# Softmax denominators in three PSUM rows per head group instead of one, in a fused attention and MLP kernel

## The chip, the cores and the metric

The kernel runs on one core of one Trainium2 chip. The metric is the device time of one execution in microseconds (us). Engines are called as in the profile: PE (TensorE matmuls), PEld (TensorE weight loads), DVE (VectorE), ACT (ScalarE), POOL (GpSimd), SP (SyncE).

## What is computed

Forgetting attention over 8 batches of 8 heads, 576 positions, head dimension 64, and then a two-layer MLP with a tanh GELU over the 4608 rows of 512 features that come out of it.

```
scores = scale * q @ k.T;  cum = cumsum(log(clip(f, 1e-4, 1)))
attn   = exp(where(causal, -1e9, scores + cum_i - cum_j) - max)
out    = (attn / (sum(attn) + 1e-9)) @ v          # per head
y      = gelu_tanh(x @ w_in) @ w_out              # x: the heads side by side
```

The kernel keeps the exponentials `pt` with keys on partitions and queries along the columns. The decay of a key is a weight per key, `w`; it multiplies the values (`vw`), and the denominator of a query is the sum over keys of `w * pt`, a matmul with the single column `w_bf` as its weights.

## The kernel before

**Head groups.** The work of attention is cut into 16 groups of 4 heads (quads), i = 0 to 15; quad i belongs to batch i // 2. A quad's exponentials lie in `pt[i % 2]`, 128 partitions x 4 heads x 1536 columns. The causal triangle is cut into six pieces by blocks of keys (`low`, 0, 1, 2, 3, `high`), of 64, 512, 448, 320, 192 and 64 query columns: 1600 columns per head.

**Steps of a quad**, by the names of the order tables:
- S.i.r (L264): scores of one of three rounds of 512 columns, matmuls at L282, with the four heads in four row strips of TensorE, and the exponential on ACT at L290.
- M.i.r (L292): the causal mask by selects on POOL (L296), one per diagonal block. M.i.2 issues two of them, first that of key block 2, then that of key block 3. m.i.r does the same on DVE (L326).
- D.i (L361): the denominators. `product` (L330, matmuls at L352) sends 6 pieces x 4 heads = 24 matmuls, the four heads in four column strips of TensorE, into PSUM row 32 * h of tile `po`: one useful row per head, 576 columns wide. For pieces 0 and `low` the weight column is repeated 32 times, so that all 32 rows of a head have a number; for the others it is one column. Then DVE transposes all 576 columns in 32 x 32 blocks from PSUM to `den` (L371), takes the reciprocal of 18 values per partition (L373), and spreads them back to 32 rows per head by a second transpose into `rb` (L375).
- V.i.x (L379): the weighted values, again 24 matmuls at L352 in the same shapes, and on DVE the product with `rb` into `xT` (L384). x = 0 and 1 are the even and odd features.

Quads 0 and 1 are done in two parts of 256 and 320 queries, D.0.p and V.0.x.p, with matmuls at L338 into tile `po_m`; they have 2 and 5 pieces.

**The order** is written out by hand. The tables FRONT, SECOND, STEADY, FLUSH and LAST (L71 on) list words that are issued in sequence; every engine takes its instructions in that order. Between the steps of attention stand pieces of the MLP for rows that are ready: F and f (second layer, L616; f sends it in four column strips of 32), I and i (first layer, L400), Q (first layer by seven products, L536). From quad 6 on, two quads go with one chunk of 512 rows, and the order around a pair is

```
S.3.0 X G.1.1.2 f.0.16 M.3.0 D.2 VW.3 f.0.12 S.3.1 M.3.1 V.2.0 f.0.13
S.3.2 M.3.2 CL.3 V.2.1 VW.4 f.0.15 S.4.0 D.3 f.0.10 V.3.0 M.4.0 CL.4
```

with 2 and 3 standing for the chunk's even quad (which was masked in the turn before) and its odd quad. So M.3.2, the last mask of the odd quad, is issued to POOL one S, one V and some f ahead of D.3.

**PSUM.** `po` is the only buffer of its pool (`psO`, L347), which D, V and some first-layer products share; `po_m` takes one of two buffers of `psM` (L334).

Of the kernel before, what the change touches and what calls it, by code (L numbers as in the profile page):

```python
# [8 lines left out]
FP32 = mybir.dt.float32  # L9
# [7 lines left out]
def kernel(  # L17
# [10 lines left out]
    nc = tc.nc  # L28

    B, H, S, D = q.shape  # L30
# [20 lines left out]
    pieces = [  # L51
        ("low", 0, 0, 64),
        (0, 64, 64, 512),
        (1, 576, 128, 448),
        (2, 1024, 256, 320),
        (3, 1344, 384, 192),
        ("high", 0, 512, 64),
    ]
    QA = 256
    split_rounds = [(1152, 384), (0, 512), (512, 320), (832, 384)]  # L60
    split_pieces = [
        [(0, 1152, 0, 256), (1, 1408, 128, 128)],
        [(0, 0, 256, 320), (3, 320, 384, 192)],
        [(1, 512, 256, 320)],
        [(2, 832, 256, 320), ("high", 1152, 512, 64)],
    ]
    LOW, HIGH = NT, NT - 1
# [1 line left out]
    ON_ACT = ()  # L69

    FRONT = """  # L71
        LP.1 LP.4 SC LP.0 WI.0 B.8.512 B.1.512 CT TK.0 CE.1 TQ.0 CE.0 B.2.512 LP.3 B.1.128 BK.0.2 B.1.512 WI.5 B.1.512 S.0.0 TK.1 M.0.0 B.1.128
        B.1.128 WI.1 WI.2 B.1.128 BK.0.1 B.3.512 H.0.2.1 B.1.128 BK.0.1 H.0.2.0 WI.3 H.0.1.0 W.0 LP.2 TQ.1 D.0.0 H.1.0.0 vw.0.0 B.1.128 B.2.512
        BK.1.1 H.1.0.1 M.1.0 H.0.1.1 B.1.512 M.0.1 vw.1.0 V.0.1.0 B.1.128 B.1.512 V.0.0.0 H.0.3.0 UT D.1.0 j.0.0.4 V.1.0.0 V.1.1.0 H.1.3.1 WI.4 WI.7
        H.0.3.1 WI.6 j.0.0.4 j.0.0.8 H.1.1.0 RJ.0.0 M.0.3 WO.0 H.1.1.1 vw.0.1 LC.1.1 D.0.1 j.0.1.8 H.1.3.0 M.1.1 WO.1 M.1.3 H.1.2.1 V.0.0.1 VW.1.1
        V.0.1.1 UW.2.1 W.1 LQ.2 H.1.2.0 J.0.2 LK.2 LK.3 WO.2 D.1.1 j.0.1.8 GJ.0.1 V.1.0.1 V.1.1.1 TK.2 J.0.3 tr WO.3 J.1.1 TQ.2 GJ.0.0 LQ.3 U.0
        J.1.3 J.1.2 J.1.0 F.0.1 f.0.3 LC.1.2 LC.1.0 f.0.2 S.2.0 TK.3 X f.0.2 PW.2.2 F.0.7 LC.1.3 F.0.1 S.2.2 f.0.2 F.0.1 TQ.3 f.0.2 LC.1.4 LQ.4 LK.5
        f.0.4 S.2.1 F.0.1 f.0.4 LV.2.1 F.0.1 LK.4 F.0.3 M.2.2 F.0.1 vw.2 m.2.1 F.0.2 CL.2 LV.2.0 S.3.0 f.0.1 M.2.0 f.0.2 D.2 f.0.3 S.3.1 TQ.4 f.0.1
        LQ.6 VW.3 f.0.4 M.3.0 f.0.1 V.2.0 TK.4 S.3.2 f.0.6 V.2.1 m.3.1 S.4.1 f.0.4 LQ.5 f.0.1 H.4.2.0 f.0.2 M.3.2 H.4.2.1 cl.3 D.3 VW.4 H.4.0.0
        M.4.2.3 H.4.0.1 V.3.1 LK.6 v.3.0 f.0.1 F.0.1 I.1.2 I.1.0 TQ.5 U.1 TK.5 TQ.6 vw.5 I.1.5 UW.2.4 I.1.1 LV.3.1 LV.3.0 I.1.3 TK.6 U.3 I.1.4 U.2  # L80
        m.4.2.2 I.1.6 I.1.7 LK.7 X F.1.1 CL.5 F.1.2 M.4.1 G.0 G.1.1.2 F.1.4 cl.4 F.1.9 S.5.0 F.1.12 UW.2.3 m.4.0 F.1.4 M.5.0 F.1.4 F.1.5 S.5.1 D.4
        F.1.5 LQ.8 F.1.2 F.1.4 S.5.2 V.4.0 f.1.1 M.5.1 M.5.2.2 M.5.2.3 LK.8 f.1.11 V.4.1 S.6.0 f.1.3 D.5 LQ.7@m.3.1 M.6.0 f.1.10 S.6.1 vw.6 f.1.1
        V.5.1 f.1.1 F.1.9 CL.6 M.6.1 F.1.2 S.6.2 m.6.2.3 f.1.1 V.5.0 f.1.4 F.1.2 m.6.2.2
    """

    SECOND = """
# [27 lines left out]
    den_pool = ctx.enter_context(tc.tile_pool(name="den", bufs=2))  # L114
    psS = ctx.enter_context(tc.tile_pool(name="psS", bufs=2, space=bass.MemoryType.PSUM))
    psO = ctx.enter_context(tc.tile_pool(name="psO", bufs=1, space=bass.MemoryType.PSUM))
    psM = ctx.enter_context(tc.tile_pool(name="psM", bufs=2, space=bass.MemoryType.PSUM))

    def many(n, shape, dtype, name):
        return [singles.tile(shape, dtype, name=f"{name}{i}") for i in range(n)]  # L120
# [11 lines left out]
    vw = many(2, [128, NT + 1, 4, D], BF16, "vw")  # L132
    pt = many(2, [128, 4, 3 * 512], BF16, "pt")
# [14 lines left out]
    w_bf = singles.tile([128, NQ, NT + 1, 4], BF16, name="w_bf")  # L148
# [12 lines left out]
    for u in range(4):  # L161
        if u not in wsum:
            n = 3 * len([x for x in wsum if x not in UNIT_LIST])
# [38 lines left out]
    parts = [(0, QA), (QA, S)]  # L202
# [127 lines left out]
    def product(i, groups, spare, part=None):  # L330
        p = pt[i % 2]
        if part is not None:
            s0, s1 = parts[part]
            po = psM.tile([128, 512], FP32, name="po_m", tag="m")  # L334
            for (key, col, q0, nq) in sorted(sum(split_pieces[1:] if part else split_pieces[:1], []), key=lambda x: HIGH if x[0] == "high" else x[0]):
                for (r0, lhsT, h) in groups:
                    w = lhsT(HIGH if key == "high" else key)
                    nc.tensor.matmul(  # L338
                        po[r0:r0 + w.shape[-1], q0 - s0:q0 - s0 + nq], w, p[:, h, col:col + nq],
                        start=(key == 0), stop=(key == (HIGH if part else 1)),  # L340
                        skip_group_check=True,
                    )
            return po[:, 0:s1 - s0]
        if spare:
            po = psS.tile([128, 2, 512], FP32, name="ps_o", tag="s").rearrange("p a n -> p (a n)")
        else:
            po = psO.tile([128, 1024], FP32, name="po", tag="po")  # L347
        for (key, col, q0, nq) in sorted(pieces, key=lambda x: {0: 0, "low": 1}.get(x[0], 2)):
            t = {"low": LOW, "high": HIGH}.get(key, key)
            for (r0, lhsT, h) in groups:  # L350
                w = lhsT(t)
                nc.tensor.matmul(  # L352
                    po[r0:r0 + w.shape[-1], 448 + q0:448 + q0 + nq], w, p[:, h, col:col + nq],
                    start=(key in (0, "low")), stop=(key in ("low", "high")),
                    skip_group_check=True,
                )
        return po[:, 448:448 + S]
# [2 lines left out]

    def denominators(i, part=None):  # L361

        def column(h):

            return lambda t: (w_bf[:, i, t, h:h + 1] if t not in (0, LOW) else
                              w_bf[:, i, t, h:h + 1].to_broadcast([128, 32]))

        po = product(i, [(32 * h, column(h), h) for h in range(4)], False, part)
        n = S if part is None else parts[part][1] - parts[part][0]
        den = den_pool.tile([128, S], FP32, name="den", tag="den")  # L370
        nc.vector.transpose(out=den[:, 0:n], in_=po)  # L371
        rec = den_pool.tile([128, S // 32], FP32, name="rec", tag="rec")
        nc.vector.reciprocal(rec[:, 0:n // 32], den[:, 0:n:32])  # L373
        rb = den_pool.tile([128, S], FP32, name="rb", tag="rb")
        nc.vector.transpose(out=rb[:, 0:n].rearrange("p (c j) -> p c j", j=32),  # L375
                            in_=rec[:, 0:n // 32].unsqueeze(2).to_broadcast([128, n // 32, 32]))
        rbs[i, part] = rb[:, 0:n]
# [398 lines left out]
    def load_values(b, half):  # L776
# [9 lines left out]
        "M": lambda i, r, *keys: mask(i, r, keys),  # L786
        "m": lambda i, r, *keys: mask_by_product(i, r, keys),
        "D": denominators,
        "V": lambda i, x, *part: attn_out(i, x, False, *part),
        "v": lambda i, x, *part: attn_out(i, x, True, *part),  # L790
# [98 lines left out]
```

## Time and profile before

| what | us |
|---|---|
| median of 3 runs (range) | 322.77 (321.95 to 322.95) |
| the profiled execution's own time | 322.02 |
| its span, first to last instruction | 320.1 |
| PE busy in it | 311.8 |
| DVE busy in it | 242.5 |
| granted TensorE clock | 1.00 throughout |

In the rows of the profile, the first number of a line of the timeline or of the chain is the start in us from the span's start, the second its length in us. "x24" is a count of instructions. "128*32" is a weight tile of 128 rows and 32 columns. What stands in brackets is idle time before the row, with what ended it. In the rows of one group, "busy, mean ns" comes before the bar's idle time.

### The profile page before, as it was taken

To read this page: it belongs to the slowest core of one execution; us is meant where nothing else is said; L and a number is where in the kernel's file an instruction comes from. 1 tells how busy PE (TensorE), PEld (TensorE's weight loads), DVE (VectorE), ACT (ScalarE), POOL (GpSimd) and SP (SyncE) were. 2 spreads that over 40 slices of the span, in tenths; PEclk is the share of its full clock that TensorE was granted. 3 is DMA by queue.
4 is the path that set the end of the run, shared out by engine and by line. 5 is a ranking of instruction groups with operands and counts; after the bars stand their busy time and mean duration, and the time that the engine had idled before them with its cause. 6 is when DMAs were issued, how large, how long until landed. Compare 5 with 4: busy or idle time off the path is not lost.

```text
span 320.1 us, 11762 instructions
## 1 busy us (share of the span) xinstructions
PE 311.8 (97%) x5301; PEld 219.1 (68%) x5318; DVE 242.5 (76%) x369; ACT 212.9 (67%) x246; POOL 109.9 (34%) x148
## 2 busy tenths in 40 slices
PE   6899999999999999999999999999999999999996
PEld 2367734545676577776788878767776786688785
DVE  7667528598878889879877987699876865597674
ACT  3766885966766876877677866787686744836610
POOL 8799541830340417311850075206610140000000
PEclk9999999999999999999999999999999999999999
DMA  7999999985253901693149411961011110100203
GB/s 127 227 197 204 208 222 223 171 153 105 51 99 100 215 9 39 137 190 72 39 97 218 84 39 44 218 137 38 5 60 40 35 39 33 35 33 2 100 33 99
DMA packets 47491, 33.41 MB, mean 104 GB/s; under 512 B 29777, under 2 KB 42193, under 8 KB 47441
## 3 DMA queue, kind: packets, MB, share of 16 engines
q0 software_dynamic: 9632, 15.99, 29.1%
q1 hardware_dynamic: 37664, 16.60, 19.4%
q8 instruction: 41, 0.67, 0.9%
q14 instruction: 10, 0.07, 0.1%
q10 hardware_dynamic: 144, 0.07, 0.1%
HBM read 36.85 MB, written 9.44 MB: 145 GB/s over the span
## 4 chain that ended last, share of the span: by engine, by line
PE 91%; DMA 3%; ACT 2%; POOL 1%; DVE 1%; issue 1%; DVEq 0%; POOLq 0%
PE ps_w L616 30%; PE ps_h L400 19%; PE po L352 9%; PE ps_s L282 9%; PE ps_q L536 8%; PE pso L685 5%; PE ps_h L436 5%; PE ps_u L484 4%; DMA v_nat<-in_v_dram 3%; PE po_m L338 1%; ACT gT L408 1%; ACT pt L290 1%; POOL v_nat L183 0%; PE ps_o L352 0%; PE ps_p L616 0%
## 5 line engine op out<-in xcount | busy, mean ns | idle before, releaser
L290 ACT ACTIVATE pt<-ps_s 128x1024 bf16<-128x1024 f32 (+2 forms) x100 | 94.2, 991 | 38.1 <-PE ps_s L282 36.4
L296 POOL TENSOR_SCALAR_AFFINE_SELECT pt<-pt 128x512 bf16<-128x512 bf16 (+3 forms) x73 | 46.2, 643 | 96.6 <-ACT pt L290 73.7
L400 PE MATMUL ps_h<-xT,w_in_sb 128*128 128x512 bf16 (+1 forms) x308 | 65.6, 357 | 1.1 <-issue 0.3
L400 PEld LDWEIGHTS <-w_in_sb 128*128 128x128 bf16 x320 | 31.2, 98 | 26.6 <-issue 0.6
L408 ACT ACTIVATE gT<-ps_h 128x1024 bf16<-128x1024 f32 x34 | 34.6, 1018 | 20.3 <-PE ps_h L400 20.0
L616 PEld LDWEIGHTS <-gT 128*32 128x32 bf16 (+1 forms) x1171 | 44.1, 97 | 5.8 <-issue 2.4
L616 PE MATMUL ps_w<-w_out_sb,gT 128*32 128x256 bf16 (+1 forms) x996 | 42.5, 273 | 0.0
L616 PEld LDWEIGHTS <-gsum 128*32 128x32 bf16 (+1 forms) x903 | 35.3, 97 | 4.0 <-issue 1.5
L282 PE MATMUL ps_s<-qT,kT 32*128 32x64 bf16 (+5 forms) x896 | 35.4, 261 | 0.9 <-DVE qT L213 0.6
L552 DVE TENSOR_TENSOR usnap<-ps_q,usnap 128x1024 f32<-128x1024 f32 x15 | 17.9, 1222 | 18.5 <-PE ps_q L536 13.2
L616 PE MATMUL ps_w<-usum,gsum 128*32 128x256 bf16 (+1 forms) x749 | 30.1, 273 | 0.0
L282 PEld LDWEIGHTS <-kT 32*128 32x128 bf16 x896 | 16.4, 92 | 17.2 <-issue 10.2
L230 POOL TENSOR_TENSOR vw<-v_nat,wT 128x1280 bf16<-128x1280 f32 (+1 forms) x12 | 27.3, 2275 | 1.4 <-DMA v_nat<-in_v_dram 1.1
L633 DVE COPY snap<-ps_w 128x512 f32<-128x512 f32 x32 | 21.8, 681 | 6.6 <-PE ps_w L616 6.5
L213 DVE STREAM_TRANSPOSE kT<-k_c 128x576 f32<-128x576 f32 x16 | 19.4, 1243 | 7.0 <-DMA k_c<-in_k_dram 7.0
L547 ACT ACTIVATE gT<-usnap 128x1024 bf16<-128x1024 f32 x15 | 15.8, 1054 | 12.1 <-DVE usnap L552 11.7
L384 DVE TENSOR_TENSOR xT<-po,rb 128x576 bf16<-128x576 f32 x26 | 19.5, 751 | 5.1 <-PE po L352 4.9
L213 DVE STREAM_TRANSPOSE qT<-q_c 128x576 f32<-128x576 f32 x16 | 19.7, 1241 | 3.7 <-DMA q_c<-in_q_dram 3.7
L352 PE MATMUL po<-pt,vw 128*32 128x64 bf16 (+4 forms) x624 | 22.4, 278 | 0.0
L206 POOL DMA_DIRECT2D k_c<-in_k_dram x16 | 9.1, 567 | 34.9 <-DVE kT L213 23.0
L352 PEld LDWEIGHTS <-vw 128*32 128x32 bf16 x672 | 14.6, 97 | 9.3 <-issue 2.6
L536 PEld LDWEIGHTS <-w_in_sb 128*128 128x128 bf16 x160 | 15.7, 98 | 2.5 <-issue 0.4
(134 smaller groups left out, 481.4 us busy)
## 6 DMA issues: line engine op xcount, KB each, us to landing
out_dram<-o_st SPq DMA_DIRECT2D x35, 256.0 KB, 2.2
k_c<-in_k_dram POOLq DMA_DIRECT2D x16, 288.0 KB, 5.6
q_c<-in_q_dram POOLq DMA_DIRECT2D x16, 288.0 KB, 6.1
v_nat<-in_v_dram SPq DMA_DIRECT2D x16, 256.0 KB, 5.3
v_nat<-in_v_dram SPq DMA_DIRECT2D x20, 128.0 KB, 5.2
v_nat<-in_v_dram POOLq DMA_DIRECT2D x8, 256.0 KB, 8.8
w_in_sb<-in_moe_w_in_dram POOLq DMA_DIRECT2D x8, 256.0 KB, 7.9
w_out_sb<-in_moe_w_out_dram POOLq DMA_DIRECT2D x4, 512.0 KB, 9.8
```

Source lines behind the costliest of these rows:

```text
L213: return nc.vector.transpose(out=dst.rearrange("p s c -> p (s c)").bitcast(FP32) .rearrange("p (t a) -> p a t", a=n), in_=src.rearrange("p ...
L230: return eng.tensor_mul(vw[i % 2][:, t0:t1], vb[:, t0:t1, h0:h0 + 4, :], wT[:, i, t0:t1, :].unsqueeze(3).to_broadcast([128, t1 - t0, 4, D]))
L282: nc.tensor.matmul(tiles[h // 2][:, h % 2, c0:c0 + nq], key_columns(i, key, h, c), qq[32 * h:32 * h + 32, q0:q0 + nq, c], start=(c == 0 an ...
L290: nc.scalar.activation(p[:, 2 * g:2 * g + 2, off:off + n], t[:, :, 0:n], AF.Exp, scale=scale)
L296: nc.gpsimd.affine_select(out=x, in_=x, compare_op=ALU.is_ge, fill=0.0, base=0, pattern=pattern, channel_multiplier=-1)
L352: nc.tensor.matmul(po[r0:r0 + w.shape[-1], 448 + q0:448 + q0 + nq], w, p[:, h, col:col + nq], start=(key in (0, "low")), stop=(key in ("lo ...
L384: nc.vector.tensor_mul(xT[:, 2 * u + x, r0 + s0:r0 + s1], po, rbs[i, part])
L400: nc.tensor.matmul(ph[:, j, n * cols:(n + 1) * cols], w_in_sb[:, dt, 128 * ft:128 * ft + 128], xT[:, dt, h0:h0 + cols], start=(dt == 0 and ...
L408: nc.scalar.activation(gelus(c, 2 * pr, 2), ph, AF.Gelu_apprx_tanh)
L536: nc.tensor.matmul(ps[:, k, HC * n:HC * n + HC], w[:, d, 128 * n:128 * n + 128], x[:, d, :], start=(first and n == 0 and d == 0), stop=(d ...
L616: nc.tensor.matmul(ps[c0:c0 + width, n, cols[0]:cols[1]], x[:, j, 128 * n + c0:128 * n + c0 + width], w[:, j, cols[0]:cols[1]], start=(fir ...
L633: copy(kept[name], ps)
```

## The change

D is written anew, with its own matmuls at L368 of the new file. The columns of a quad are folded in three: queries 384 to 575, 192 to 383 and 0 to 191 all go to the same 192 columns of `po`, in rows 2, 1 and 0 of each head's strip of 32. The folds are sent in that order, each over the pieces that reach it: the last fold first, with the weight column repeated 32 times (so it writes rows 0 to 31), then the middle one with the column repeated twice (rows 0 and 1), then the first with one column (row 0). For quads 0 and 1 each part is folded in two, to 128 or 160 columns. The pieces are cut where they cross a fold: widths per head are 192, 192, 192, 192, 64 in the last fold, 192, 192, 128 in the middle one and 64, 128, 64 in the first, 1600 columns as before, in 11 sets of four matmuls instead of 6. The transpose to `den` then covers 192, 128 or 160 columns; the reciprocal reads three values (two in the parts) out of each block of 32; `rb` is the same as before. V and the rest of the kernel are unchanged. The table FRONT has the same words in the same order and is only broken into lines differently.

```diff
     def denominators(i, part=None):
-        def column(h):
-            return lambda t: (w_bf[:, i, t, h:h + 1] if t not in (0, LOW) else
-                              w_bf[:, i, t, h:h + 1].to_broadcast([128, 32]))
-        po = product(i, [(32 * h, column(h), h) for h in range(4)], False, part)
-        n = S if part is None else parts[part][1] - parts[part][0]
-        den = den_pool.tile([128, S], FP32, name="den", tag="den")
-        nc.vector.transpose(out=den[:, 0:n], in_=po)
+        s0, s1 = (0, S) if part is None else parts[part]
+        n, folds = s1 - s0, 3 if part is None else 2
+        width = n // folds
+        p = pt[i % 2]
...
+        for r in reversed(range(folds)):
+            a, z = s0 + width * r, s0 + width * r + width
+            parts_of = [(key, col + max(q0, a) - q0, max(q0, a), min(q0 + nq, z)) for (key, col, q0, nq) in todo if max(q0, a) < min(q0 + nq, z)]
+            m = 32 if r == folds - 1 else r + 1
+            for k, (key, col, qa, qz) in enumerate(parts_of):
+                t = {"low": LOW, "high": HIGH}.get(key, key)
+                for h in range(4):
+                    nc.tensor.matmul(
+                        po[32 * h:32 * h + m, qa - a:qz - a], w_bf[:, i, t, h:h + 1].to_broadcast([128, m]),
+                        p[:, h, col:col + qz - qa],
+                        start=(k == 0), stop=(k == len(parts_of) - 1),
+                        skip_group_check=True,
+                    )
+        den = den_pool.tile([128, S // 3], FP32, name="den", tag="den")
+        nc.vector.transpose(out=den[:, 0:width], in_=po[:, 0:width])
         rec = den_pool.tile([128, S // 32], FP32, name="rec", tag="rec")
-        nc.vector.reciprocal(rec[:, 0:n // 32], den[:, 0:n:32])
+        nc.vector.reciprocal(rec[:, 0:n // 32].rearrange("p (r c) -> p r c", r=folds),
+                             den[:, 0:width].rearrange("p (c x) -> p x c", x=32)[:, 0:folds, :])
```

More of the change, by code (lines that the diff above doesn't have):

```diff
@@ L71 @@
     FRONT = """
[L72 to L83, printed above, removed]
+        LP.1 LP.4 SC LP.0 WI.0 B.8.512 B.1.512 CT TK.0 CE.1 TQ.0 CE.0 B.2.512 LP.3 B.1.128 BK.0.2 B.1.512 WI.5 B.1.512 S.0.0 TK.1 M.0.0 B.1.128 B.1.128 WI.1 WI.2 B.1.128 BK.0.1 B.3.512 H.0.2.1 B.1.128 BK.0.1 H.0.2.0 WI.3 H.0.1.0 W.0 LP.2 TQ.1 D.0.0 H.1.0.0 vw.0.0 B.1.128 B.2.512 BK.1.1 H.1.0.1 M.1.0 H.0.1.1 B.1.512 M.0.1 vw.1.0 V.0.1.0 B.1.128 B.1.512 V.0.0.0 H.0.3.0 UT D.1.0 j.0.0.4 V.1.0.0 V.1.1.0 H.1.3.1 WI.4 WI.7 H.0.3.1 WI.6 j.0.0.4 j.0.0.8 H.1.1.0 RJ.0.0 M.0.3 WO.0 H.1.1.1 vw.0.1 LC.1.1 D.0.1 j.0.1.8 H.1.3.0 M.1.1 WO.1 M.1.3 H.1.2.1 V.0.0.1 VW.1.1 V.0.1.1 UW.2.1 W.1 LQ.2 H.1.2.0 J.0.2 LK.2 LK.3 WO.2 D.1.1 j.0.1.8 GJ.0.1 V.1.0.1 V.1.1.1 TK.2 J.0.3 tr WO.3 J.1.1 TQ.2 GJ.0.0 LQ.3 U.0 J.1.3 J.1.2 J.1.0 F.0.1 f.0.3 LC.1.2 LC.1.0 f.0.2 S.2.0 TK.3 X f.0.2 PW.2.2 F.0.7 LC.1.3 F.0.1 S.2.2 f.0.2 F.0.1 TQ.3 f.0.2 LC.1.4 LQ.4 LK.5 f.0.4 S.2.1 F.0.1 f.0.4 LV.2.1 F.0.1 LK.4 F.0.3 M.2.2 F.0.1 vw.2 m.2.1 F.0.2 CL.2 LV.2.0 S.3.0 f.0.1 M.2.0 f.0.2 D.2 f.0.3 S.3.1 TQ.4 f.0.1 LQ.6 VW.3 f.0.4 M.3.0 f.0.1 V.2.0 TK.4 S.3.2 f.0.6 V.2.1 m.3.1 S.4.1 f.0.4 LQ.5 f.0.1 H.4.2.0 f.0.2 M.3.2 H.4.2.1 cl.3 D.3 VW.4 H.4.0.0 M.4.2.3 H.4.0.1 V.3.1 LK.6 v.3.0 f.0.1 F.0.1 I.1.2 I.1.0 TQ.5 U.1 TK.5 TQ.6 vw.5 I.1.5 UW.2.4 I.1.1 LV.3.1 LV.3.0 I.1.3 TK.6 U.3 I.1.4 U.2 m.4.2.2 I.1.6 I.1.7 LK.7 X F.1.1 CL.5 F.1.2 M.4.1 G.0 G.1.1.2 F.1.4 cl.4 F.1.9 S.5.0 F.1.12 UW.2.3 m.4.0 F.1.4 M.5.0 F.1.4 F.1.5 S.5.1 D.4 F.1.5 LQ.8 F.1.2 F.1.4 S.5.2 V.4.0 f.1.1 M.5.1 M.5.2.2 M.5.2.3 LK.8 f.1.11 V.4.1 S.6.0 f.1.3 D.5 LQ.7@m.3.1 M.6.0 f.1.10 S.6.1 vw.6 f.1.1 V.5.1 f.1.1 F.1.9 CL.6 M.6.1 F.1.2 S.6.2 m.6.2.3 f.1.1 V.5.0 f.1.4 F.1.2 m.6.2.2
@@ L361, in denominators @@
     def denominators(i, part=None):
-        def column(h):
-            return lambda t: (w_bf[:, i, t, h:h + 1] if t not in (0, LOW) else
-                              w_bf[:, i, t, h:h + 1].to_broadcast([128, 32]))
-        po = product(i, [(32 * h, column(h), h) for h in range(4)], False, part)
-        n = S if part is None else parts[part][1] - parts[part][0]
-        den = den_pool.tile([128, S], FP32, name="den", tag="den")
-        nc.vector.transpose(out=den[:, 0:n], in_=po)
+        s0, s1 = (0, S) if part is None else parts[part]
+        n, folds = s1 - s0, 3 if part is None else 2
+        width = n // folds
+        p = pt[i % 2]
+        if part is None:
+            po = psO.tile([128, 1024], FP32, name="po", tag="po")
+        else:
+            po = psM.tile([128, 512], FP32, name="po_m", tag="m")
+        todo = sorted(pieces if part is None else sum(split_pieces, []), key=lambda x: {"low": -1, "high": HIGH}.get(x[0], x[0]))
+        for r in reversed(range(folds)):
[13 more added lines that the diff above has]
+        nc.vector.transpose(out=den[:, 0:width], in_=po[:, 0:width])
         rec = den_pool.tile([128, S // 32], FP32, name="rec", tag="rec")
-        nc.vector.reciprocal(rec[:, 0:n // 32], den[:, 0:n:32])
+        nc.vector.reciprocal(rec[:, 0:n // 32].rearrange("p (r c) -> p r c", r=folds),
+                             den[:, 0:width].rearrange("p (c x) -> p x c", x=32)[:, 0:folds, :])
         rb = den_pool.tile([128, S], FP32, name="rb", tag="rb")
```

## The prediction

> **What bounds the kernel now.** I read the page's busy times and chain first, then busy time by stretch, then the list of who waited for whom, and last the instructions around single D blocks.
>
> ```profile
> span 320.1 us, 11762 instructions
> PE 311.8 (97%) x5301; PEld 219.1 (68%) x5318; DVE 242.5 (76%) x369; ACT 212.9 (67%) x246; POOL 109.9 (34%) x148
> PE 91%; DMA 3%; ACT 2%; POOL 1%; DVE 1%; issue 1%; DVEq 0%; POOLq 0%
> ```
> TensorE is busy for 311.8 of 320.1 us and holds 91% of the chain that ended last; DVE, whose work the change cuts, holds 1% of it. An average can hide a stage where DVE sets the pace, so I ask for stretches. In the next view the columns are the window, its length, and the busy us (instructions) of PE, PEld, DVE, ACT and POOL, then the granted clock, the DMA share and GB/s.
>
> ```profile
> 18.00:62.00 44.00, 43.60 (x748) 26.09 (x745) 25.91 (x39) 32.29 (x37) 27.12 (x38) 1.00 1.09 204
> 62.00:100.00 38.00, 37.74 (x603) 23.25 (x603) 33.22 (x47) 26.87 (x30) 11.55 (x16) 1.00 0.51 104
> 100.00:131.00 31.00, 30.95 (x620) 20.72 (x621) 27.14 (x44) 21.78 (x26) 11.03 (x12) 1.00 0.39 85
> 131.00:232.00 101.00, 100.79 (x2122) 76.74 (x2124) 83.45 (x119) 75.63 (x83) 39.09 (x48) 1.00 0.49 104
> ```
> From 18 to 232 us PE is idle for 0.40 + 0.26 + 0.05 + 0.21 = 0.92 us in all. Even where DVE is fullest (33.22 of 38 us), PE does not wait for it. D of quads 2 to 13 falls into these stretches, so a shorter DVE step has almost nothing to give back there. A busy PE could still be a slow one, so I test its pace next.
>
> ```profile
> 135.15 1.75 PE ps_q L536 x16
> 143.21 3.45 PE ps_h L400 x16
> 149.15 0.68 PE po L352 x24
> 157.55 0.80 PE po L352 x24
> ```
> These are rows of the chain. A matmul of 512 columns takes 3.45 / 16 = 0.2156 us, one of 256 takes 1.75 / 16 = 0.1094 us; so a column costs 0.415 ns and each matmul 3.2 ns besides. In a D or V block four heads run side by side, so that 24 matmuls are 6 sets over 1600 columns: 1600 x 0.415 + 6 x 3.2 = 683 ns, and the chain shows 0.68. The block at 157.55 differs by 0.12 us: it follows scores, which use row strips. A D block runs at TensorE's own pace, and none is held up by DVE.
>
> **The change, part by part.** *What DVE saves.*
>
> ```profile
> L371 DVE STREAM_TRANSPOSE den<-po 128x576 f32<-128x576 f32 x14 | 10.9, 781 | 5.8 <-PE po L352 5.8
> L371 DVE STREAM_TRANSPOSE den<-po_m 128x320 f32<-128x320 f32 x2 | 1.0, 513 | 0.0
> L371 DVE STREAM_TRANSPOSE den<-po_m 128x256 f32<-128x256 f32 x2 | 0.9, 429 | 0.5 <-PE po_m L338 0.5
> ```
> From 256 to 576 columns the transpose grows by 781 - 429 = 352 ns, 1.1 ns a column. By that line 192 columns take 0.36 us (0.42 saved, 14 times), 128 take 0.29 (0.14 saved, twice) and 160 take 0.32 (0.19 saved, twice): 5.9 + 0.7 = 6.6 us of DVE. The reciprocal and the second transpose keep their sizes; I cost them as unchanged. What is late next is nothing: DVE waited before D (5.8 us of idle time before these transposes, ended by PE), and will wait a little more. V.x.0 needs `po` from the transpose, but 10 or more groups of f stand between, and PE's idle time above shows no wait there. I take 0 for the gain, with 0 to 0.9 us as its bounds (all of PE's idle time from 18 to 232).
>
> *What PE pays for narrower sets.* The columns stay 1600 per head, the sets grow from 6 to 11: 5 x 3.2 = 16 ns per D, 14 times: 0.22 us. For this the loads of a narrow set must still hide.
>
> ```profile
> 149.20 0.12 PEld L352 LDWEIGHTS <-w_bf 128*1 128x1 bf16 x8
> L352 PEld LDWEIGHTS <-w_bf 128*1 128x1 bf16 x224 | 4.4, 84 | 3.4
> 156.86 0.69 PE L282 MATMUL ps_s<-qT,kT 32*128 32x64 bf16 x24
> L282 PE MATMUL ps_s<-qT,kT 32*128 32x64 bf16 x352 | 16.4, 190 | 0.0
> ```
> In D at 149 us the loads for two successive sets, eight of 84 ns, lie within 0.12 us: the second set's loads began at most 36 ns after the first's, over a set of 64 columns (27 ns of columns). In the scores of round 0, six sets (64, 448, 64, 64, 448, 64 columns: two narrow ones in a row) take 0.69 us to the end of the last, 0.50 to its start (0.69 - 0.19), where the five before it have 1088 x 0.415 = 0.45. That leaves 10 ns a set, so the price of the 70 extra sets lies between 3.2 and 10 ns: 0.22 to 0.70 us. I take 0.22, since the D block itself fits it.
>
> [...]
>
> *A mask that is now needed earlier.* This is the largest term. Before, key block 3, whose diagonal POOL masks last, came as the fifth set, after 512 + 64 + 448 + 320 columns, 1344 x 0.415 + 4 x 3.2 = 0.57 us into D. Now the last fold goes first, and key block 3 is its fourth set: after 3 x (192 x 0.415 + 3.2) = 0.25 us. Its columns 1344 to 1535 hold the diagonal; the three sets ahead of it lie beyond theirs. For the odd quads the select ends close to D:
>
> ```profile
> 123.25 1.23 POOL L296 TENSOR_SCALAR_AFFINE_SELECT pt<-pt 128x512 bf16<-128x512 bf16 x2 [1.47 <-ACT pt L290]
> 124.06 0.75 PE L352 MATMUL po<-pt,w_bf 128*32 128x512 bf16 x16
> 156.59 1.23 POOL L296 TENSOR_SCALAR_AFFINE_SELECT pt<-pt 128x512 bf16<-128x512 bf16 x2 [0.94 <-ACT pt L290]
> 157.48 0.87 PE L352 MATMUL po<-pt,w_bf 128*32 128x512 bf16 x24
> 223.73 1.23 POOL L296 TENSOR_SCALAR_AFFINE_SELECT pt<-pt 128x512 bf16<-128x512 bf16 x2 [0.94 <-ACT pt L290]
> 224.62 0.86 PE L352 MATMUL po<-pt,w_bf 128*32 128x512 bf16 x24
> ```
> These are quads 7, 9 and 13; quad 11 lies between and repeats quad 9. How soon PE goes on after a select, D.1.0 shows, which waited for one:
>
> ```profile
> 16.44 0.63 POOL L296 TENSOR_SCALAR_AFFINE_SELECT pt<-pt 128x512 bf16<-128x512 bf16 x1
> 16.89 0.22 PE po_m L338 x4
> 17.12 0.23 PE po_m L338 x4
> ```
> The select ends at 17.07, the next set begins at 17.12: 0.05 us. So D.7 can go on at 123.25 + 1.23 + 0.05 = 124.53, but comes to its fourth set at 124.06 + 0.25 = 124.31: 0.22 us lost. D.9: 157.87 against 157.73, 0.14 lost; D.13: 225.01 against 224.87, 0.14; D.11 the same. Sum 0.22 + 3 x 0.14 = 0.64 us. Before, the fifth set came at 124.63, 158.05 and 225.19, after the mask each time. POOL's spans are rough, so the bounds of this term are 0 and about 1.1 us (0.1 us more at each of the four). Behind the waiting matmul stand f, V.x.0 and all else of PE, which has no idle time to take it up. The select starts when ACT ends the exponential of a round that PE sent 3 us earlier, so a PE that waits here doesn't delay the mask in turn. Of the other quads, the nearest case and a typical even one are D.3 and D.8:
>
> ```profile
> 59.82 1.22 POOL L296 TENSOR_SCALAR_AFFINE_SELECT pt<-pt 128x512 bf16<-128x512 bf16 x2
> 60.92 0.83 PE L352 MATMUL po<-pt,w_bf 128*32 128x512 bf16 x17
> 132.09 1.23 POOL L296 TENSOR_SCALAR_AFFINE_SELECT pt<-pt 128x512 bf16<-128x512 bf16 x2 [2.02 <-ACT pt L290]
> ```
> D.3 can go on at 61.09 and comes there at 61.17: no wait, with 0.08 us to spare. D.8 begins at 149 us, over 15 us after its mask.
>
> *The front.*
>
> ```profile
> 20.47 1.00 POOL L296 TENSOR_SCALAR_AFFINE_SELECT pt<-pt 128x512 bf16<-128x512 bf16 x2 [0.21 <-ACT pt L290]
> 21.05 0.70 PE L338 MATMUL po_m<-pt,w_bf 128*32 128x320 bf16 x20
> 20.57 1.24 DVE usum L416
> 21.85 1.03 PE ps_h L436 x8
> ```
> D.1.0 waited for its second set until 17.12; now a third set of 128 columns follows: + 0.06 us. In D.0.1 piece `high` is now the fifth of nine sets, due at 21.05 + 4 x 0.07 = 21.33; its select ends at 20.47 + 1.00, so it starts at 21.52, and the rest takes 0.27: end 21.79, where it was 21.05 + 0.52 = 21.57. The next work waited for DVE's copy until 21.81 anyway, and needs 0.1 for the change of strips: + 0.05. D.1.1: four sets more, one of them with 32 columns: + 0.03. D.0.0 has one more set, ahead of a wait of PE for DVE at 12.8 us: 0.
>
> *The sum:* 0.22 + 0.64 + 0.06 + 0.05 + 0.03 = 1.0 us, without any gain. The profiled execution took 322.02 us (span 320.1 and 1.9 around it) and would take 323.0. It is 0.75 us below the median of 322.77; I put the 1.0 us on the median: **323.8 us**, 0.3% slower, at the edge of what a measurement of this kernel can tell from no change (about 0.3%, 0.97 us).
>
> **The rivals.** *The mask is there in time.* If POOL releases PE 0.15 to 0.2 us before its recorded end, or the sets reach key block 3 that much later, only 0.3 to 0.4 us are left: 323.1, within 0.3%. For it: POOL's spans are rough. Against: D.1.0 fits them to 0.05 us.
>
> *DVE's relief reaches the end of the kernel.* That is the side of a gain. It decides where PE stands waiting for a DVE step that queues behind `den`. If all 6.6 us arrived, it would be 322.77 + 1.0 - 6.6 = 317.2 us; with PE's idle time of 0.92 us as the limit it is 322.9. Against it: after 18 us PE has one wait for DVE on the chain, the copy at 20.57, which itself waited for PE; and in the list of PE's waits, DVE ends only these three, all in the first 13 us:
>
> ```profile
> PE cum_ps L742 <- DVE f_all L721: 1.3, 1, 1.3
> PE idle_ps L255 <- DVE idle L705: 1.3, 1, 1.3
> PE ps_s L282 <- DVE qT L213: 0.6, 1, 0.6
> ```
>
> *The loads show after all* when several narrow sets follow one another (64, 192, 192, 128, 64, 128, 64 at the end of a D). If a set can't be shorter than a load, 84 ns, each D pays 3 x 57 + 2 x 31 + 6 x 4 = 257 ns, 14 times 3.6 us, with the fronts 3.8: 322.77 + 0.8 + 3.8 = 327.4. [...] Against it: the eight loads in 0.12 us and the two narrow sets in a row.
>
> *A change of weight width drains TensorE* as the change of strips does (0.12 us, the 0.80 against the 0.68 above). Weights of two columns are new; 32 to 2 and 2 to 1 are two changes per D, 14 x 2 x 0.12 = 3.4 us: 327.2. Against it: the D block of 0.68 us already goes from 32 columns to 1, and shows no gap. [...]
>
> **How the numbers follow.** The forecast, a loss of 0.6 to 1.4 us, 323.4 to 324.2: 0.57, of which 0.35 beyond 0.97 us and 0.22 within. The mask in time, 323.1: 0.28, all within 0.3%. DVE's relief: 0.05, counted as faster, although its limit of 322.9 says it is generous. Loads that show 0.05, drains 0.05, both slower. So faster 0.05, same 0.50, slower 0.45: the likeliest single case lies on the line between the last two. The range 322.5 to 324.8 takes in the forecast with the bounds of its two largest terms (323.8 + 0.48 for dearer sets + 0.46 for longer waits is 324.7) and the first rival; it leaves out the loads, the drains, a large gain, and a little for the scatter of the runs.
>
> **What the profile after would show.** PE busy up by about 0.3 us and idle time or a longer first set in D.7, D.9, D.11, D.13 of 0.1 to 0.2 us, ended by POOL (L296). `den` rows of 128x192 at about 0.36 us, DVE busy about 236. D blocks of even quads at 0.70 us; were they at 0.8 or 0.95, drains or loads are the cause. No wait of D for POOL in the odd quads speaks for the first rival. A median under 322.4 means that I have missed a wait for DVE.

## The result: 6.9 us slower, and what the profile after shows

| kernel | median us (range, runs) | ratio to before, 95% interval |
|---|---|---|
| before | 322.84 (321.95 to 323.50, 6) | |
| the change | 329.69 (328.41 to 331.74, 6) | 1.0229 (1.0203 to 1.0255) |

The ratios, here and below, aren't quotients of the medians (here that would be 1.0212). One run further down, of 330.48 us, counts as slow, being over 1.5% above the fastest of its kernel, and is left out of its ratio.

The profiled execution of the changed kernel took 330.35 us, its span is 328.5. First the lines of its page that answer to those of before: the span, busy times by engine, the granted clock in 40 slices, the instruction queue (packets, MB, share), the chain by engine.

```profile
span 328.5 us, 12419 instructions
PE 319.2 (97%) x5638; PEld 225.1 (69%) x5638; DVE 236.8 (72%) x369; ACT 212.7 (65%) x246; POOL 108.7 (33%) x148
PEclk9999999999997999999999999999999999999999
q8 instruction: 44, 0.72, 0.9%
PE 83%; DMA 8%; ACT 3%; POOL 2%; DVE 2%; issue 1%; DVEq 0%; ACTq 0%
```

VectorE has 5.7 us less to do, as planned, and TensorE is still the bound. Two things are new: one slice of the clock is no longer full, and there are 44 packets of instructions, where the page of before has

```profile
q8 instruction: 41, 0.67, 0.9%
```

Then the D blocks themselves, in the chain of the changed kernel, an even quad and an odd one (start, length):

```profile
155.50 0.69 PE po L368 x44
164.16 0.94 PE po L368 x32
```

The even one takes 0.69 us with 44 matmuls, where it took 0.68 with 24. The narrow sets cost what was forecast, and neither loads nor a drain show inside them. The odd one, D.9, holds two waits that overlap: it stopped in its third set, from 164.26 to 164.43 us, for a reason that the next section gives, and its fourth set began at 164.47, 0.05 us after the mask's select had ended. So where are 7 us? The same view for the stretch of quads 4 and 5:

```profile
86.38 0.81 PE po L368 x44
87.18 1.31 PE ps_w L621 x11
...
92.47 0.22 PE ps_w L621 x3
92.69 0.48 issue
93.16 0.48 PE ps_w L621 x9
93.64 0.63 PE po L368 x40
...
96.24 0.57 PE po L341 x15
96.80 1.73 issue
98.53 0.30 PE po L341 x6
```

TensorE stops in the middle of a run of f (92.69) and in the middle of V.5.1 (96.80), in blocks that the change didn't touch. "issue" means that it waited for nothing that the profile shows: no semaphore, no engine, no buffer. The same view of the kernel before has no such row between 84 and 99 us; the same run of f and the same V.5.1 stand there in one piece each:

```profile
90.72 0.44 PE ps_w L616 x12
...
96.60 0.68 PE po L352 x24
```

And shortly after the longer gap the clock halves (the windows view, PE's columns first, the granted clock after POOL's):

```profile
99.10:102.50 3.40, 3.40 (x31) 1.91 (x34) 2.17 (x4) 0.03 (x1) 0.00 (x0) 0.50 0.16 52
```

3.4 us at 0.50 cost about 1.7 us (half of the 3.4, my estimate). The half clock begins 0.57 us after the end of the stand of 1.73 us; that the one brings the other on is not shown by this trace alone.

### The profile page after: what moved, and what is told of

Its sections match the earlier page's. It is cut to its first block, busy times and chain, and to the rows that moved or that the text cites. A ratio compares the mean times of both kernels' runs of the same rounds, so it can differ in the third digit from the quotient of the medians.

```text
span 328.5 us, 12419 instructions
## 1 busy us (share of the span) xinstructions
PE 319.2 (97%) x5638; PEld 225.1 (69%) x5638; DVE 236.8 (72%) x369; ACT 212.7 (65%) x246; POOL 108.7 (33%) x148
## 4 chain that ended last, share of the span: by engine, by line
PE 83%; DMA 8%; ACT 3%; POOL 2%; DVE 2%; issue 1%; DVEq 0%; ACTq 0%
PE ps_w L621 30%; PE ps_h L405 19%; PE ps_s L271 9%; PE ps_q L541 8%; PE po L341 6%; PE ps_u L489 4%; DMA v_nat<-in_v_dram 4%; PE po L368 3%; DMA w_out_sb<-in_moe_w_out_dram 3%; PE pso L690 2%; PE idle_ps L244 1%; ACT pt L279 1%; DMA f_all<-in_f_dram 1%; POOL v_nat L172 1%; ACT gT L413 1%
## 5 line engine op out<-in xcount | busy, mean ns | idle before, releaser
L285 POOL TENSOR_SCALAR_AFFINE_SELECT pt<-pt 128x512 bf16<-128x512 bf16 (+3 forms) x73 | 45.2, 629 | 98.5 <-ACT pt L279 75.5
L405 PE MATMUL ps_h<-xT,w_in_sb 128*128 128x512 bf16 (+1 forms) x320 | 66.9, 358 | 0.2 <-ACT gT L413 0.2
L621 PE MATMUL ps_w<-usum,gsum 128*32 128x256 bf16 (+1 forms) x749 | 31.2, 273 | 0.6 <-issue 0.5
L271 PEld LDWEIGHTS <-kT 32*128 32x128 bf16 x896 | 16.4, 94 | 17.1 <-issue 10.4
L341 PE MATMUL po<-pt,vw 128*32 128x64 bf16 (+4 forms) x624 | 23.2, 278 | 2.3 <-issue 2.3
L341 PEld LDWEIGHTS <-vw 128*32 128x32 bf16 x672 | 15.6, 97 | 11.2 <-issue 5.6
```

What stands on the lines that cost most here:

```text
L271: nc.tensor.matmul(tiles[h // 2][:, h % 2, c0:c0 + nq], key_columns(i, key, h, c), qq[32 * h:32 * h + 32, q0:q0 + nq, c], start=(c == 0 an ...
L285: nc.gpsimd.affine_select(out=x, in_=x, compare_op=ALU.is_ge, fill=0.0, base=0, pattern=pattern, channel_multiplier=-1)
L341: nc.tensor.matmul(po[r0:r0 + w.shape[-1], 448 + q0:448 + q0 + nq], w, p[:, h, col:col + nq], start=(key in (0, "low")), stop=(key in ("lo ...
L405: nc.tensor.matmul(ph[:, j, n * cols:(n + 1) * cols], w_in_sb[:, dt, 128 * ft:128 * ft + 128], xT[:, dt, h0:h0 + cols], start=(dt == 0 and ...
L621: nc.tensor.matmul(ps[c0:c0 + width, n, cols[0]:cols[1]], x[:, j, 128 * n + c0:128 * n + c0 + width], w[:, j, cols[0]:cols[1]], start=(fir ...
```

## What the gaps have in common: the supply of instructions

TensorE has 11286 instructions in the changed kernel's records, 11276 of them loads and matmuls; 0.72 MB in 44 packets is 16.4 KB and about 256 instructions a packet. I took the trace's instruction packets and the places between 20 and 320 us at which TensorE's stream stood still, and counted instructions up to each gap. These are the gaps of over 0.2 us inside a run of equal matmuls that no semaphore and no missing record explains (at 198.3, in D.11, a mask is waited for as well). They are counted from the start of the last instruction to the start of the next, so that the last matmul's own run is in them: the chain's 1.73 us is 2.03 here. Steps of about 0.3 us where TensorE goes from one kind of matmul to another stand in both kernels and are left out.

```
TensorE stops  goes on  at instruction    last packet   goes on after its end
 64.18          64.89    7 x 256 + 193     62.23-63.44   1.45
 92.41          93.16   10 x 256 + 193     90.85-91.74   1.42
 96.51          98.54   11 x 256 + 193     96.32-97.27   1.27
156.46         156.70   18 x 256 + 193    154.07-155.30  1.40
198.32         198.75   27 x 256 + 193    195.57-197.39  1.36
202.07         202.48   28 x 256 + 193    199.86-201.01  1.47
233.38         233.59   32 x 256 + 193    230.94-232.14  1.45
```

Each gap stands at the border of a block of 256 instructions, and ends 1.3 to 1.5 us after a packet of instructions has landed. So does the shorter stop in D.9 (at 21 x 256 + 193, 1.3 us after a packet). Where instructions are dense and no loads are under way in this trace, the packet of the next block mostly starts 0.1 to 1.1 us after TensorE enters the block ahead of it, and takes 0.9 to 1.8 us. With the 1.4 us from its end to its use, a block must last some 2.4 to 4.3 us (my estimate, the sums of the least and the most), or TensorE runs dry. How long does one last? Three blocks of before and three of after that hold a whole D each, by the windows view (PE matmuls and PEld loads in brackets add up to a block, with a few that reach across its borders):

```profile
148.11:151.90 3.79, 3.79 (x137) 2.89 (x129) 3.69 (x7) 3.02 (x5) 0.78 (x2) 1.00 0.02 4
155.66:159.27 3.61, 3.61 (x138) 2.80 (x130) 2.94 (x6) 2.48 (x3) 2.68 (x3) 1.00 0.02 5
190.47:194.23 3.76, 3.76 (x134) 2.54 (x130) 3.12 (x6) 1.94 (x2) 3.69 (x5) 1.00 0.02 4
```

```profile
153.44:156.70 3.26, 3.26 (x135) 2.86 (x128) 3.19 (x6) 3.23 (x4) 0.00 (x0) 1.00 0.12 38
187.64:190.75 3.11, 3.11 (x135) 2.86 (x128) 3.04 (x6) 3.08 (x4) 0.00 (x0) 1.00 0.08 22
223.06:226.15 3.09, 3.09 (x136) 2.85 (x125) 2.99 (x7) 3.04 (x4) 0.04 (x1) 1.00 0.02 5
```

Before, a block with a D in it lasted 3.6 to 3.8 us, and, with 1.4 us from a packet's end to its use, the next was ready 0.4 to 1.2 us ahead of need. The new D puts 88 instructions where 48 stood, into the same 0.69 us, and such a block lasts 3.1 to 3.3 us: the next one is ready just in time or late. No reserve is built up where it could be seen: TensorE spent 15.7 us in the block from 137.75 to 153.44, whose successor's packet had come from 136.88 to 138.10, and no further packet started before 154.07.

The longest gap has a second cause. For 93.0 to 96.2 us, and then for 96.1 to 97.5, the view of the DMA queues (packets, MB, share of the 16 engines) of the changed kernel:

```profile
q0 software_dynamic: 204, 0.43, 80.9%
```

```profile
q0 software_dynamic: 90, 0.17, 67.1%
q8 instruction: 1, 0.02, 4.2%
```

TensorE entered the block at 93.16, but its successor's packet came only at 96.32, after three microseconds in which the k and q loads of coming quads (q0) had the DMA engines busy. The gap at 92.41 is of the same kind: TensorE had entered the block ahead at 88.67, the packet came only at 90.85, and from 88.0 to 90.6 us the view shows

```profile
q0 software_dynamic: 116, 0.26, 70.9%
```

Ahead of the gap at 64.18 the packet came late as well (block entered at 58.75, packet from 62.22). I call this theory A: the supply of instructions is short where TensorE's instructions are dense, and loads in that place make it late.

The rivals: B, the folds themselves (a mask needed earlier, the largest term of the prediction); C, narrow sets that show their loads or drain TensorE; and that the number of instructions costs, not their density.

## The experiments

All are compared with the kernel before on the same chip, whose median was 322.41 to 322.48 us.

### The sets without the folds

```diff
-        for (key, col, q0, nq) in sorted(pieces, ...):
+        for (key, col, q0, nq) in cut(sorted(pieces, ...), 0, S, folds):
```

On the kernel before, in D alone: `cut` splits the pieces at queries 192 and 384, and nothing is folded ("..." stands for the sort's key). The cut sets of block 0 and of `low` start their sums anew, which changes the denominators.

> The kernel before with D cut into the same 11 sets of four matmuls (7 extra per part pair as in the change), but nothing folded: every set writes its own columns, key block 3 stays late, VectorE transposes 576 columns as before. Theory A (supply of instructions: TensorE reads its instructions in blocks of 256, 41 of them before and 44 after, and a block that holds the 88 instructions of the new D is used up in 3.1 to 3.5 us, about as fast as the next one comes): the count and the density are those of the change, so most of the 6.85 us stays, 327 to 331 us, with idle time of PE and its loads put down to 'issue' in the middle of V or f blocks. Theory B (the folds themselves, by the mask that is needed earlier): the mask wait is gone, only the sets' fixed cost is left, 323.1 us. Theory C (narrow sets show their loads or drain TensorE inside D): D blocks of 0.8 to 1.1 us in the chain in place of 0.68, every time, and 326 to 330 us.

Measured: 328.51 us, ratio 1.0172 (1.0128 to 1.0216). Its chain:

```profile
90.16 0.22 PE ps_w L622 x3
90.38 0.58 issue
...
94.04 0.57 PE po L358 x15
94.61 2.55 issue
97.16 0.40 PE po L358 x6
```

With neither a fold nor a shorter transpose, the loss and the gaps are there, in the same words of the order. Theory A gave 327 to 331, B 323.1. D blocks of even quads take 0.69 us in this chain (at 153.78 and 188.35), not C's 0.8 to 1.1. The added PE instructions alone bring 6.1 us, most of the loss or all of it.

### The mask late again

```diff
-        for r in reversed(range(folds)):
+        for r in range(folds):
-            m = 32 if r == folds - 1 else r + 1
+            m = 32 if r == 0 else folds - r
```

and one reciprocal per fold, from row `folds - 1 - r`.

> The changed kernel with the folds sent in the other order (queries 0 to 191 first, in row 2; 384 to 575 last, in row 0), and one reciprocal per fold, so that key block 3 comes at the end of D again. Same number and widths of matmuls. Theory B: the waits of D.7, D.9, D.11 and D.13 for POOL go, 0.6 us of the change's 6.85: about 329.0 us if they are a part beside the rest, 323 if they are all of it. Theory A: the supply is as short as with the change: 327 to 331 us, and the idle time 'issue' of PE stays.

Measured: 328.30 us (324.41 to 330.48), ratio 1.0149 (1.0105 to 1.0193). The median lies where theory A had it, and the profiled execution still stands for 0.99 and 2.00 us at the two borders, at 91.74 and 96.38; so B isn't the cause of most of it. The ratio is lower than the change's 1.0229 by more than B's 0.6 us, and the two intervals don't meet; how much of that is the mask stays open, for single runs scatter over 6 us, where those of before scatter over 2. The seven gaps of the table last from 0.21 to 2.03 us from start to start, the longest of them among loads; that the cost of a gap differs so from run to run may well be the reason, but that was not tried by itself.

### Fewer instructions around D, in both kernels

```diff
-        "f": lambda c, n: out_part(c, n, 1),
+        "f": lambda c, n: out_part(c, n),
```

> The changed kernel with every f (second layer in four strips of 32 columns, 8 instructions per 256 columns) sent as F (128 columns, 2 instructions per 256 columns). About 2800 PE instructions fewer, same arithmetic; more changes of strips, 0.1 us each. To be read against the kernel before with the same edit, of the same call. Theory A: with few instructions per us around D the blocks last and the change costs only 0.3 to 1.2 us over that kernel, no slower clock and no issue gaps. Theory C: D itself is dear, so the difference stays at 4 to 7 us. Theory B: 0.6 us.

> The kernel before with every f sent as F, as the base for the run above. All theories: a few us slower than the kernel before by the changes of strips (some 30 more of 0.1 us: 325 to 327 us), or about equal; its own time is not what tells, the difference to the changed kernel with wide f is.

Measured: the change 326.20 us, ratio 1.0129 (1.0103 to 1.0154); before 326.32 us, ratio 1.0126 (1.0100 to 1.0152). Between the two lie -0.1 us, give or take about 1 us with four runs each: of the 6.9 us of the change nearly all is gone. Both are 3.8 to 3.9 us slower than the kernel before, which the expected 325 to 327 us covers; that the changes of strips are the reason was not taken apart. With 33 packets of instructions,

```profile
q8 instruction: 33, 0.54, 0.7%
```

blocks last long enough (the shortest of the changed kernel's after 20 us lasts 5.0 us), and within that 1 us 44 matmuls in D cost no more than 24. This speaks plainly against C, which had 4 to 7 us here. B's 0.6 us can't be told from nothing.

### As many instructions in a sparse place

```diff
-        spans = [(n0, CH)] if n0 + CH <= RING else [(n0, HC), ((n0 + HC) % RING, HC)]
+        spans = [(n0, HC), ((n0 + HC) % RING, HC)]
```

> The kernel before with each 512-column matmul of the first layer (I, i) sent as two of 256 columns with its own weight load: some 510 PE instructions more, nearly as many as the change adds (640), but in stretches where an instruction lasts about 54 ns and a block of 256 over 10 us. If the number of instructions is what costs (fetching them, their DMA traffic), it should be about 5 us slower: 327 to 329 us. Theory A says density counts, not number: only the fixed 3.2 ns of some 250 matmuls, 0.8 us: 322.8 to 323.8 us, no issue gaps inside V or f.

Measured: 323.39 us, ratio 1.0030 (1.0016 to 1.0043): 0.9 us for 512 instructions, about the fixed 3.2 ns of 256 added matmuls (0.8 us), and far from 5. So density costs, not number alone. One part of the expectation failed: the profiled execution has a gap inside V.5.1, which in the kernel before is in one piece.

```profile
96.65 0.43 PE po L352 x12
97.08 0.55 issue
97.63 0.43 PE po L352 x12
```

It stands at a border of blocks too: TensorE entered the block ahead of it at 91.72, and the next packet came only at 95.26, among the same loads. The added instructions had moved the borders. So where a border falls counted here beside density, with loads near: 0.55 us.

### VectorE's part alone

```diff
-        den = den_pool.tile([128, S], FP32, name="den", tag="den")
-        nc.vector.transpose(out=den[:, 0:n], in_=po)
+        den = den_pool.tile([128, S // 3], FP32, name="den", tag="den")
+        nc.vector.transpose(out=den[:, 0:width], in_=po[:, 0:width])
```

> The VectorE half of the change alone: TensorE's D as before (24 matmuls, 576 columns), but VectorE transposes 192 columns (128 or 160 in the parts) and takes the reciprocal in the change's pattern. The folds that it then reads are not there, so the denominators of most queries are left out. VectorE loses 5.7 us of busy time as in the change. All theories that put the cost on TensorE: no gain, 321.9 to 322.9 us (within 0.2% of before). If VectorE's relief were worth something on the path, it would show here alone: down to 320 us or less.

Measured: 322.07 us, ratio 0.9986 (0.9974 to 0.9998). DVE's busy time is down by 4.9 us on its page (the expectation had said 5.7), and its transposes are as short as the change's:

```profile
PE 311.9 (98%) x5301; PEld 219.1 (69%) x5318; DVE 237.6 (74%) x369; ACT 213.0 (67%) x246; POOL 110.6 (35%) x148
L373 DVE STREAM_TRANSPOSE den<-po 128x192 f32<-128x192 f32 x14 | 5.3, 380 | 5.9 <-PE po L352 5.9
```

So 5 us of VectorE are worth about 0.4 us (0.1 to 0.8 by the interval).

### The loads out of the dense stretch, in both kernels

```diff
-  ... F.1.5 LQ.8 F.1.2 ... LK.8 f.1.11 ... LQ.7@m.3.1 M.6.0 ... m.6.2.2
+  ... F.1.5 F.1.2 ... f.1.11 ... M.6.0 ... m.6.2.2 LQ.7 LK.8 LQ.8
```

> The changed kernel with the three loads LQ.7, LK.8, LQ.8 taken out of the dense stretch between D.4 and V.5 (issued at 87 to 93 us) and put at the end of FRONT. Theory A says that the two longest gaps there (0.48 and 1.73 us) came because the instruction block waited behind these loads on the DMA engines, and that the gap of 1.73 us then brought 3.4 us of half clock, 1.7 us more. So 3 to 4 us should go, with the slower clock: 325 to 327 us, clock 1.0; short gaps elsewhere stay. If loads have nothing to do with it: 328 to 331 us, gap and slower clock as before.

> The kernel before with the same three loads moved, as the base for the run above. Expected by all theories: 322 to 323.5 us, about that of the kernel before, if no step waits for the later loads.

Measured: the change 324.69 us, ratio 1.0062 (1.0041 to 1.0084); before 322.61 us, ratio 1.0003 (0.9990 to 1.0016). About 5 us of the loss go, without a single instruction of TensorE changed; I had expected 3 to 4. The chain of the changed kernel with the loads later, at the same words as above, has no "issue" row, and the clock is full:

```profile
91.17 0.44 PE ps_w L632 x12
91.62 0.69 PE po L379 x44
92.31 1.09 PE ps_w L632 x40
93.40 0.57 PE ps_s L282 x13
93.97 0.22 PE ps_w L632 x4
94.19 0.68 PE po L352 x24
```

```profile
PEclk9999999999999999999999999999999999999999
```

The mean clock is 0.998 to 1.000 in the four runs, where five of the six runs of the change have 0.994 or 0.995. So the larger part of the 6.9 us is the meeting of a dense stretch with bulk loads, and what came with it (the half clock among it). Three gaps at borders of blocks are left in this trace, of 0.4, 0.4 and 0.8 us (at 192.3, 196.1 and 227.4).

### Both edits, and then one f sent wide

The first kernel has the loads later and the mask late; the second has one more edit, in STEADY:

```diff
-        ... VW.4 f.0.15 S.4.0 D.3 ...
+        ... VW.4 F.0.15 S.4.0 D.3 ...
```

> The changed kernel with both edits tried so far: the three loads later, and the folds sent in the other order so that key block 3 comes last. Beside the run with the loads alone (324.69 us, 2.2 above before): theory B's four waits for POOL, measured there as 0.20 (D.7), 0.14 (D.9) and 0.13 us (D.13), with D.11 about the same, are gone: 324.1 us. What is left then is theory A's short gaps (about 1.3 us in that profile) and the sets' fixed cost (0.25 us). If the waits are swallowed by the gaps (a wait for the mask gives the next instruction block time to come), less than 0.6 us goes.

> The kernel of the run above, with one word of STEADY sent wide: the 15 f ahead of S.4.0 and D.3 as F (90 PE instructions fewer in each of three turns, 0.1 us more each for one more change of strips). Theory A: the blocks around D of the odd quads last again, most of the short gaps between 150 and 232 us go (about 1 us), 0.3 us is paid: 323.0 to 323.6 us, level with before within 0.3%. If the gaps stay or only the 0.3 us shows: 324.0 to 324.6 us.

Measured: 324.75 us, ratio 1.0066 (1.0042 to 1.0091), and 323.35 us, ratio 1.0034 (1.0017 to 1.0051). The late mask brought nothing that can be measured, though the waits of D for POOL are gone from that trace. That they were swallowed by gaps is one reading. The two profiled executions tell of another: with the late mask TensorE passes an early border of blocks (2 x 256 + 193) 0.8 us later than without (28.56 against 27.76 us), and the last one (43 x 256 + 193) only 0.1 us later (317.15 against 317.01), so between them it gained 0.7 us. That is about what B had said, but the gaps fall elsewhere in the two, so it stays open. The wide f brought 1.4 us by the medians, as expected, though the two intervals overlap: with 90 instructions fewer per turn, one gap at a border of blocks is left after 20 us (0.4 us at 126.8). The remaining 0.9 us was not taken apart; the sets' fixed cost (0.25 us, from 3.2 ns a set) and three more changes of strips (0.3 us, from about 0.1 us each), both my estimates, are in it. No version with the folds beats the kernel before, and the run with VectorE's part alone says how little there would be to win.

## Why the prediction was wrong, point by point

- *What bounds the kernel: TensorE, with nothing for VectorE to give.* Right, and shown: VectorE's part alone gives 0.4 us, within the bounds of 0 to 0.9.
- *VectorE saves 6.6 us.* It saves 5.7. A transpose of 192 columns takes 0.38 us, not 0.36:

```profile
L375 DVE STREAM_TRANSPOSE den<-po x14: 371/382/384, 52.8 to 270.5; 128x192 f32<-128x192 f32 x14
```

- *Narrower sets cost 16 ns a D, 0.22 us, at most 0.70.* **This is the step that failed.** The D block did come out at 0.69 us, so as the time of D it was right. As the price of 640 more instructions it was wrong by some 6 us (the sets alone, without folds, cost 6.1): in the profile after, TensorE stops at borders of 256 instructions for 0.2 to 2.0 us, so the supply of instructions has a cost, which the sum put at nothing, and I asked only what TensorE makes of them once they are there. The page of before already had the row of the instruction queue, 41 packets; I passed it over, and a test by blocks would have shown that the next block was ready only 0.4 to 1.2 us ahead of need. Taking 0.5 us out of a block of 3.6 uses most of that up, or all of it. My bounds came from the pace within a D, which says nothing of when the next block comes.
- *A mask needed earlier: 0.22 us in D.7, 0.14 each in D.9, D.11 and D.13.* In the trace with the loads moved, D.7 stands 0.20 us, D.9 0.14 and D.13 0.13 for POOL; D.11 meets a border of blocks at the same place, so its share can't be told. The reading by spans was right. In the time it can't be told: putting the mask back made no difference with the loads later (1.0066 against 1.0062), and without that a larger one than these waits can explain (1.0149 against 1.0229). The term left out D.2, which stood 0.3 us for VectorE's part of its mask (L315), in the profile of the change alone.
- *The front: 0.14 us.* Not tested by itself. In the profile of the change, TensorE is about 0.8 us later than before by the end of it; but the first D already starts 1.6 us later (13.41 against 11.85 us), so this can't be put down to the D blocks.
- *The rivals.* "The loads show" gave 327.4 us and "a drain" 327.2: near the measured time, for reasons that are not there, since D takes 0.69 us and costs nothing that can be measured among wide f. A number that fits is no proof; the D rows that the prediction had named as the test refuted both. "DVE's relief" fell too.
- *The range* left out the one resource that I hadn't priced. With the two rivals near 327 at 0.05 each, the chance of a loss of several us, 0.10, was far too low.
- *What the profile after would show.* DVE's 236 us (236.8) and even D blocks at 0.70 us (0.69) came as said; PE's busy time rose by 7.4 us instead of 0.3.

In the changed kernel's profile the seven gaps of the table make 4.8 us from start to start, or about 4.1 less the usual step of 0.1 us each, of the 8.4 us by which its span is longer; my estimates for the rest are 1.7 for the half clock, about 0.5 for the waits for POOL, 0.25 for the sets, 0.3 to 0.5 for the wait of D.2, and 0.7 for the start. This is an account of one execution; its parts aren't independent.

## What to carry to other kernels

Count the instructions per us as a resource of its own: add up TensorE's loads and matmuls in the densest stretch, see how long a block of them (256 here) lasts, and compare that with the time in which the trace shows the next packet of instructions to come. Here the sets added in D alone cost 6.1 us, where I put their own length at 0.25, and its two gaps shown above (0.58 and 2.55 us) stood in blocks that the edit didn't touch; about 5 us of the change's 6.9 went when three bulk loads issued there were moved. The sign was a gap of the kind "issue" in the middle of a run of equal matmuls, with no semaphore before it (0.48 and 1.73 us); the tests were sending the same columns in fewer instructions (326.20 us against 326.32) and moving the loads (324.69).

## What the hardware showed that I had not expected

- TensorE's instructions arrived 256 at a time (11286 in 44 packets, and seven gaps at borders of 256), and it went on 1.3 to 1.5 us after a packet's end in each of the seven.
- A stand of 1.73 us in an otherwise full stream was followed, 0.6 us after its end, by 3.4 us at half the clock. It isn't needed for a long run: one of the six runs of the change shows a mean clock of 1.000 and took 331.74 us, the longest.
- With all f sent wide, 24 or 44 matmuls over the same 1600 columns made no difference beyond about 1 us of noise (326.32 and 326.20 us).
